# Casting GpSimd loads for r and v, regrouped input weights and a new issue order in a fused RWKV-7 and squared-ReLU MLP kernel

## The chip, the cores and the metric

The kernel runs on one core of a Trainium2 chip. The metric is the device time of one execution in microseconds. An execution is called fast or slow: slow is one more than 1.5% above the fastest of the same kernel. The profile of the kernel before that is read below was taken in an execution of 303.0 us that counted as slow in its own first set (fastest 296.8 us); in later sets nearly all its runs between 297 and 303 us counted as fast. Spans read from that profile are therefore some us longer than those of a typical fast execution (medians of about 300 to 302 us in the later sets), and the text says where that matters.

Ratios are the mean time of one kernel's fast runs over that of the other's in the same rounds on the same chip, so they are not quite the ratios of the medians quoted beside them.

In the views PE is TensorE, PEld its weight loads, DVE VectorE, ACT ScalarE, POOL GpSimd and SP SyncE; a q behind a name is the engine's sequencer, which issues DMAs. L284 is line 284 of that run's kernel. A line of the groups ends with busy us, mean ns of one instruction, and the idle time before it with what ended it. A line of the waits ends with the total us, the number of waits and the longest.

## The reference

The reference runs a recurrent attention over 768 steps for 4 x 8 heads of width 40, and feeds the result to an MLP.

```python
for t in range(S):
    y[:, :, t] = np.einsum('bhd,bhde->bhe', rt, state)
    Sa = np.einsum('bhde,bhe->bhd', state, at)
    state_decay = state * wt[:, :, None, :] - np.einsum('bhd,bhe->bhde', Sa, bt)
    state = state_decay + np.einsum('bhd,bhe->bhde', vt, kt)
# x: (3072 tokens, 320), made of y
h = x @ w_in              # 320 x 2048
r = np.maximum(h, 0.0)
out = (r * r) @ w_out     # 2048 x 320
```

## The kernel before

The kernel cuts the 768 steps into chunks of 64, and handles a chunk for two batch entries at a time: 24 groups of 128 tokens. A full group goes through 65 small operations (loads, decay sums, transposes, triangular products, state update, MLP, store). A list scheduler in the kernel places the operations of all groups from tables of priorities (`PLACE`, `FIRST`, `LAST`) and emits one instruction stream per engine. ScalarE and VectorE work their streams in order: in the trace before, all 264 ScalarE and 260 VectorE instructions of the groups start in exactly the emitted order.

All inputs come in on SyncE's queue, but for the MLP weights (GpSimd) and the first group's k and b (ScalarE). A group has twelve SyncE issues: two halves each for w, k, b, a and v, one for r, and the store of the group's output.

```python
def load(name, dst, step, src, other, deps):
    eng = "ACT" if g == 0 and name in ("LK", "LB") else "SP"
    q_ = nc.scalar if eng == "ACT" else nc.sync
    def f():
        for be in range(2):                      # two batch entries: two DMAs
            h = 1 - be if other else be
            q_.dma_start(out=V(dst, step * be, [(40, 8), (1, 40)], 64 * h, 64), in_=tok(src, b0 + be))
    add(name, g, eng, 1.3, f, deps, dma=1.05)
...
load("LV", vf, 0, v, True, [...])                # fp32 staging tile
nc.sync.dma_start(out=rf[:], in_=src)            # r, fp32 staging tile
...
nc.gpsimd.tensor_copy(out=V(rb, ...), in_=V(rf, ...))              # RC: cast r
nc.gpsimd.tensor_copy(out=V(vm, 512 * be, ...), in_=V(vf, ...))    # VC0, VC1: cast v
```

The first MLP product reads its stationary weights with a step of 16 columns, because hidden unit 16*partition + block makes the output weights contiguous to load:

```python
mm(out=V(p, 512 * s + 128 * i, [(1, 128)]), lhsT=V(WIN[x], blk, [(16, 128)]),
   rhs=xt[:, 128 * x:128 * x + 128], start=False, stop=i == 3 and x > 0)
```

## Time and profile before

| | before |
|---|---|
| time, median of the first 4 runs | 301.0 us (296.8 to 304.6) |
| span in the profile | 301.3 us |
| TensorE busy | 265.5 us, 88% |
| GpSimd busy | 131.9 us, 44% |
| SyncE issues in the trace | 284, their lengths sum to 232 us |
| DMA engines, mean share in the middle | 0.6 |

The prediction below shows the lines of this profile one by one. One reading that it did not make is added here. It is the timeline of SyncE in a calm part of the kernel before; the columns are start, length, and what was issued how often in a row.

```profile
112.35 1.28 SPq L284 DMA_DIRECT2D Vf<-in_v_dram  x2
113.68 0.63 SPq L295 DMA_DIRECT2D Rf<-in_r_dram  x1
114.35 2.42 SPq L284 DMA_DIRECT2D KBf<-in_k_dram  x2
116.87 1.54 SPq L284 DMA_DIRECT2D Af<-in_a_dram  x2
```

Each issue begins within 0.1 us of the end of the last. SyncE does not stop for a buffer or a result here; it issues without a break. Counted over the trace in stretches of 20 us, it is issuing for 18.0 to 19.1 us of each, from the first to 240 us. Its pace can be set against TensorE's: from 40 to 240 us it makes 226 issues in 199 us, twelve per 10.6 us, while TensorE in its steady part needs 10.3 us for a group. So SyncE is, by a little, the slower of the two and cannot catch up once it is late. The page's busy shares cannot show this: issuing does not count as busy. Most issues take about 0.63 us, but 63 of the 284 take over 1 us, and these make the pace; in 47 of the 63 none of the semaphores (the counters of finished work) that the issue waits for changed meanwhile, so they are no plain waits for tiles. What lengthens them stays open.

### The profile page before, as it was taken

How to read it: one execution, taken by the hardware profiler on the slowest of the kernel's cores; microseconds unless marked ns; L12 is line 12 of the kernel's file. 1: busy time of each engine (PE TensorE's matmuls, PEld its weight loads, DVE VectorE, ACT ScalarE, POOL GpSimd, SP SyncE). 2: the span in 40 equal slices, each digit the busy share in tenths (PEclk: the TensorE clock that was granted, in tenths of full speed). 3: DMA queues.
4: the chain of work that ended last, by engine and by line, in shares of the span. 5: the costliest groups of instructions: out<-in, count | busy, mean ns of one | idle time of the engine just before them, and what ended most of it. 6: DMA issues, size and time to landing. Idle time of an engine off the chain costs nothing.

```text
span 301.3 us, 13557 instructions
## 1 busy us (share of the span) xinstructions
PE 265.5 (88%) x5928; PEld 224.5 (75%) x5928; DVE 185.0 (61%) x300; ACT 147.5 (49%) x265; POOL 131.9 (44%) x245
## 2 busy tenths in 40 slices
PE   0775999985997899999999699999999889999980
PEld 0455798875886788888888688888888778888860
DVE  7235667384565557767766557766767657875520
ACT  1443164653435266556546436645644635656340
POOL 2763533853554263763644344654546325510000
PEclk9999999999697999999999979999999999999996
DMA  8899976755656566665565656555546562000000
GB/s 118 132 154 198 201 125 98 119 115 104 114 114 108 95 110 125 113 119 98 108 124 108 119 106 117 107 113 105 103 101 112 109 125 55 29 24 6 28 29 32
DMA packets 134011, 31.02 MB, mean 103 GB/s; under 512 B 127232, under 2 KB 133376, under 8 KB 133952
## 3 DMA queue, kind: packets, MB, share of 16 engines
q1 hardware_dynamic: 131184, 27.21, 48.7%
q0 software_dynamic: 656, 2.62, 4.7%
q8 instruction: 46, 0.75, 1.0%
q10 hardware_dynamic: 2112, 0.33, 0.7%
q14 instruction: 13, 0.11, 0.1%
HBM read 28.84 MB, written 3.93 MB: 109 GB/s over the span
## 4 chain that ended last, share of the span: by engine, by line
PE 62%; DMA 16%; ACT 7%; SPq 6%; issue 4%; POOL 1%; DVE 1%; ACTq 0%; POOLq 0%
PE hp L567 16%; PE fo L585 13%; DMA Wf<-in_w_dram 10%; SPq L284 5%; PE hp L558 4%; DMA out_dram<-OSB 4%; ACT RL L572 3%; PE sx L497 3%; PE cs L316 2%; PE kt L380 2%; PE vt L508 2%; PE cp L426 2%; PE eb L426 2%; PE x L463 2%; PE x L441 2%
## 5 line engine op out<-in xcount | busy, mean ns | idle before, releaser
L572 ACT ACTIVATE RL<-hp 128x1024 bf16<-128x1024 f32 x48 | 49.0, 1021 | 37.9 <-PE hp L567 37.7
L585 PE MATMUL fo<-WOUT,GT 128*128 128x320 bf16 x384 | 61.6, 305 | 1.0 <-DVE GT L576 1.0
L567 PE MATMUL hp<-XT,WIN 128*128 128x128 bf16 x768 | 62.1, 236 | 0.0
L349 POOL TENSOR_TENSOR KB<-KBf,EXN 128x320 bf16<-128x320 f32 x47 | 40.9, 875 | 44.1 <-ACT EXN L322 31.5
L567 PEld LDWEIGHTS <-WIN 128*128 128x128 bf16 x768 | 54.6, 151 | 3.7 <-issue 0.6
L576 DVE TENSOR_TENSOR GT<-RL 128x1024 bf16<-128x1024 bf16 x48 | 34.8, 726 | 26.1 <-ACT RL L572 26.0
L585 PEld LDWEIGHTS <-GT 128*128 128x128 bf16 x384 | 35.8, 100 | 13.4 <-DVE GT L576 1.4
L355 POOL TENSOR_TENSOR A<-Af,EXE 128x320 bf16<-128x320 f32 x24 | 20.7, 863 | 48.6 <-ACT EXE L338 43.6
L430 DVE TENSOR_TENSOR EBM<-eb,MASK 128x1024 bf16<-128x1024 f32 x24 | 29.3, 1223 | 7.6 <-PE eb L426 6.7
L430 DVE TENSOR_TENSOR CPM<-cp,MASK 128x1024 bf16<-128x1024 f32 x24 | 29.2, 1217 | 4.2 <-PE cp L426 4.0
L384 DVE COPY KBT<-kt 128x1024 bf16<-128x1024 bf16 x24 | 16.6, 691 | 23.4 <-PE kt L380 23.2
L590 ACT ACTIVATE OSB<-fo 128x320 f32<-128x320 f32 x24 | 10.5, 436 | 36.4 <-DMA out_dram<-OSB 23.6
L365 POOL CAST VM<-Vf 64x320 bf16<-64x320 f32 x48 | 21.6, 451 | 11.1 <-DMA Vf<-in_v_dram 8.8
L454 ACT ACTIVATE UZ<-x 64x320 bf16<-64x320 f32 x48 | 20.7, 431 | 10.8 <-PE x L449 8.9
L308 POOL TENSOR_TENSOR LLO<-LNW 128x320 bf16<-128x320 f32 x24 | 17.3, 720 | 16.1 <-ACT LNW L300 15.9
L300 ACT ACTIVATE LNW<-Wf 128x320 f32<-128x320 f32 x24 | 11.2, 465 | 23.3 <-DMA Wf<-in_w_dram 23.3
L558 PE MATMUL hp<-XT,WIN 64*128 64x128 bf16 x384 | 22.1, 235 | 0.0
L468 ACT ACTIVATE VM<-x 64x320 bf16<-64x320 f32 x48 | 20.6, 429 | 2.7 <-PE x L463 2.1
L338 ACT ACTIVATE EXE<-ce 128x328 f32<-128x328 f32 x24 | 10.6, 444 | 22.0 <-PE ce L333 20.0
L322 ACT ACTIVATE EXN<-cs 128x640 f32<-128x640 f32 x24 | 16.8, 700 | 8.9 <-PE cs L316 6.9
L489 DVE TENSOR_TENSOR STB<-st,GLM 128x640 bf16<-128x640 f32 x22 | 18.1, 824 | 4.2 <-PE st L483 4.2
L501 DVE COPY SB<-sx 128x640 bf16<-128x640 bf16 x22 | 10.8, 491 | 15.0 <-PE sx L497 15.0
(83 smaller groups left out, 480.3 us busy)
## 6 DMA issues: line engine op xcount, KB each, us to landing
Vf<-in_v_dram SPq DMA_DIRECT2D x48, 80.0 KB
Wf<-in_w_dram SPq DMA_DIRECT2D x48, 80.0 KB
Af<-in_a_dram SPq DMA_DIRECT2D x48, 80.0 KB
Rf<-in_r_dram SPq DMA_DIRECT2D x24, 160.0 KB
out_dram<-OSB SPq DMA_DIRECT2D x24, 160.0 KB
KBf<-in_k_dram SPq DMA_DIRECT2D x46, 80.0 KB
KBf<-in_b_dram SPq DMA_DIRECT2D x46, 80.0 KB
WOUT<-in_moe_w_out_dram POOLq DMA_DIRECT2D x2, 640.0 KB, 8.6
```

The costliest lines, as they stand in the source:

```text
L349: (nc.vector if g == 0 and be else nc.gpsimd).tensor_tensor(out=V(kb, 512 * be, [(64, 8), (1, 40)]), in0=V(kbf, 320 * be, [(40, 8), (1, 40)]),
L355: nc.gpsimd.tensor_tensor(out=V(at, 0, [(64, 8), (1, 40)]), in0=V(af, 0, [(40, 8), (1, 40)]), in1=V(exe, 0, [(40, 8), (1, 40)]), op=ALU.mult)
L365: nc.gpsimd.tensor_copy(out=V(vm, 512 * be, [(64, 8), (1, 40)], h, 64), in_=V(vf, 0, [(40, 8), (1, 40)], h, 64))
L430: nc.vector.tensor_tensor(out=V(dst, 0, [(64, 16), (1, 64)]), in0=V(psum(key, g), 0, [(64, 16), (1, 64)]), in1=V(MASK, 0, [(0, 16), (1, 64 ...
L454: nc.scalar.activation(out=V(uz, 320 * be, [(1, 320)], 64 * be, 64), in_=V(psum("x", g), 0, [(1, 320)], 64 * be, 64), func=ACTF.Copy, scal ...
L468: nc.scalar.activation(out=V(vm, 512 * be, [(64, 8), (1, 40)], 64 * be, 64), in_=V(psum("x", g), 0, [(40, 8), (1, 40)], 64 * be, 64), func ...
L489: nc.vector.tensor_tensor(out=V(stb, 0, [(128, 8), (64, 2), (1, 40)]), in0=V(psum("st", g), 0, [(40, 8), (0, 2), (1, 40)]), in1=V(glm, 0, ...
L558: mm(out=V(p, 512 * s + 128 * i, [(1, 128)]), lhsT=V(WIN[1 + s], blk, [(16, 128)], 64 * s, 64), rhs=xt[64 * s:64 * s + 64, 128 + 128 * s:2 ...
L567: mm(out=V(p, 512 * s + 128 * i, [(1, 128)]), lhsT=V(WIN[x], blk, [(16, 128)]), rhs=xt[:, 128 * x:128 * x + 128], start=False, stop=i == 3 ...
L572: nc.scalar.activation(out=rl[:], in_=psum(f"hp{hf}", g)[:], func=ACTF.Relu)
L576: nc.vector.tensor_tensor(out=gt[:], in0=rl[:], in1=rl[:], op=ALU.mult)
L585: mm(out=p[:, 0:320], lhsT=gt[:, 512 * s + 128 * i:512 * s + 128 * i + 128], rhs=WOUT[:, DM * blk:DM * blk + DM], start=blk == 0, stop=blk ...
```

## The change

The intent has three parts. Casting DMAs issued by GpSimd bring r and v straight into their bf16 tiles, so the fp32 staging tiles and the GpSimd casts go away, and SyncE has nine issues per group instead of twelve. The input weights are copied once on chip into contiguous columns. The issue order was searched anew, with 3 tiles for r and 4 for v. The tile of r also loses its padding: heads of 40 columns lie side by side, and the products that transpose r step by 40 columns. The cuts below are marked by three dots.

```diff
-PERIOD = 68.08
+PERIOD = 28.01
... all of PLACE, FIRST, LAST, STAY, and the PE and GpSimd entries of WINDOW are new ...
-    RB = ring("RB", 2, 512)
+    RB = ring("RB", NR, 344)          # NR = 3
-    VM = ring("VM", 3, 1024)
+    VM = ring("VM", NV, 1024)         # NV = 4
...
-        load("LV", vf, 0, v, True, [...])
-            nc.sync.dma_start(out=rf[:], in_=src)
+            nc.gpsimd.dma_start(out=rb[:, 0:320], in_=src)
-            nc.gpsimd.tensor_copy(out=V(rb, 0, ...), in_=V(rf, 0, ...))
-                nc.gpsimd.tensor_copy(out=V(vm, 512 * be, ...), in_=V(vf, 0, ...))
+            nc.gpsimd.dma_start(out=V(vm, 512 * be, [(64, 8), (1, 40)], h, 64), in_=tok(v, b0 + be))
...
-   lhsT=V(WIN[x], blk, [(16, 128)])
+   lhsT=WIN[x][:, 128 * blk:128 * blk + 128]
...
-    init("wi3", "DVE", 0.65, lambda: nc.vector.tensor_copy(out=WIN[2][0:64, :], in_=WIN[1][64:128, :]), ["wi1"])
+    def regroup(eng, i, src, p0, q0, n):
+        o = V(WIN[i], 0, [(128, 16), (1, 128)], p0, n)
+        x = V(WRAW[src], 0, [(1, 16), (16, 128)], q0, n)
+        ...
+    init("wp0", "ACT", 1.9, regroup("ACT", 0, 0, 0, 0, 128), ["wi0"])
+    init("wp1", "DVE", 2.2, regroup("DVE", 1, 1, 0, 0, 128), ["wi1"])
+    init("wp2", "ACT", 1.9, regroup("ACT", 2, 2, 64, 64, 64), ["wi2"])
+    init("wp3", "DVE", 2.2, regroup("DVE", 2, 1, 0, 64, 64), ["wi1"])
```

## The prediction

The forecast's sum is 12.7 + 9 + 1 - 1 = about 22 us, and 299.2 - 22 = 277 us. Its 56 ns are those of the transposes in the trace before. That the strided loads hold back the hp matmuls was the conclusion from this trace, 151 against 103 ns for the loads and 72.5 against 56 ns for the matmuls. In the paragraph that is cut most, "such issues" are DMA issues of GpSimd. The first rival's 1.5 us for an issue of 512 short runs is a supposition, and no trace showed it.

> **What bounds the kernel now.** I read the page first: the busy shares, then the forty slices.
>
> ```profile
> PE 265.5 (88%) x5928; PEld 224.5 (75%) x5928; DVE 185.0 (61%) x300; ACT 147.5 (49%) x265; POOL 131.9 (44%) x245
> ...
> PE   0775999985997899999999699999999889999980
> ...
> PEclk9999999999697999999999979999999999999996
> DMA  8899976755656566665565656555546562000000
> ```
>
> TensorE is the only engine near its span. It has three weak stretches: the first four or five slices (7.5 us each), where the DMA engines are the full ones; slices 10 to 13; and slice 23. In the two later ones the granted clock drops as well. To size them I cut the trace into windows of 10 us.
>
> ```profile
> 70.00:80.00 10.00, 7.05 (x137) 6.29 (x136) 4.21 (x7) 3.13 (x6) 3.97 (x9) 0.71 0.61 113
> ...
> 130.00:140.00 10.00, 10.00 (x251) 8.60 (x249) 7.23 (x11) 6.26 (x11) 5.08 (x11) 1.00 0.59 107
> ```
>
> The columns are the busy times of PE, PEld, DVE, ACT and POOL, then clock, DMA share and GB/s. A full window does 251 matmuls. From 60 to 110 us the five windows do 226+137+232+146+230 = 971 instead of 1255, so 284/25.1 = 11.3 us are lost; from 160 to 180, 363 instead of 502, 5.5 us; from 220 to 250, 713 instead of 753, 1.6 us. Up to 40 us there are 396 matmuls, 1.6 of the 24 groups of 247, worth 16.5 us, so the start costs about 23.5 us. So far that is 42 us lost; the last 10 us, with 37 matmuls, lose several more.
>
> The rest is a steady state in which the chain of waits stays on TensorE and repeats every 10.30 us:
>
> ```profile
> 125.01 1.16 PE hp L567 x16
> 126.17 0.45 PE sx L497 x8
> ...
> 131.25 0.45 PE vt L508 x8
> ...
> 133.27 0.45 PE kt L380 x8
> ...
> 135.31 1.16 PE hp L567 x16
> ```
>
> The columns are start, length, and what. The reader should compare two rates. The transposes sx, vt and kt are 128x128 weights with 128 moving columns, and take 0.45/8 = 56 ns each. The MLP matmuls hp of line 567 have exactly the same shape and take 1.16/16 = 72.5 ns. The weight loads, kept apart by shape, say why:
>
> ```profile
> L567 PEld LDWEIGHTS <-WIN 128*128 128x128 bf16 x768 | 54.6, 151 | 3.7 <-issue 0.6
> ...
> L558 PEld LDWEIGHTS <-WIN 64*128 64x128 bf16 x384 | 16.6, 151 | 1.0 <-issue 0.5
> L380 PEld LDWEIGHTS <-KB 128*128 128x128 bf16 x192 | 13.1, 103 | 3.3 <-POOL KB L349 2.0
> L508 PEld LDWEIGHTS <-VM 128*128 128x128 bf16 x192 | 13.1, 102 | 1.3
> ```
>
> WIN is read with a step of 16 elements (32 bytes) and a load takes 151 ns; contiguous loads of the same shape take 102 and 103 ns.
>
> [...] The trace has such issues only for the MLP weights, 0.57 to 0.64 us each with long rows; it shows none with 512 short runs. [...]
>
> **The change part by part.**
> *Regrouped weights.* Contiguous loads should let line 567 run at 56 ns: per group of tokens 32 x (72.5 - 56) = 0.53 us. Line 558 (64 rows, two row halves side by side) takes 0.28/8 = 35 ns; if a pair reaches the 56 ns of one full matmul it takes 28, so 16 x 7 = 0.11 us at most. I take 0.62 us per group, a period of 9.68 us, and 24 x 0.62 = 14.9 us. All of it lies on TensorE; some 85% falls in stretches where TensorE sets the pace, 12.7 us, and the rest only pays if the waits there shrink too. It adds four regroup copies once, by the kernel's own plan 1.9 + 1.9 us on ScalarE and 2.2 + 2.2 us on VectorE, and drops one of 0.69 us. They fall near 30 us, where the DMA engines are the limit; I charge 1 us.
> *r and v by GpSimd.* GpSimd loses the casts and gains three issues per group:
>
> ```profile
> L365 POOL CAST VM<-Vf 64x320 bf16<-64x320 f32 x48 | 21.6, 451 | 11.1 <-DMA Vf<-in_v_dram 8.8
> ...
> L360 POOL CAST RB<-Rf 128x320 bf16<-128x320 f32 x24 | 11.3, 471 | 4.2 <-DMA Rf<-in_r_dram 4.1
> ...
> L654 POOL DMA_DIRECT2D WIN<-in_moe_w_in_dram x3 | 1.9, 642 | 0.0
> ```
>
> That is 32.9 us off and 72 x 0.64 = 46 us on, if the cost is like that of the weights: GpSimd goes from 132 to 145 us, half of the span, beside TensorE and not on the path. Per group it has 6.0 us of work in a period of 9.7.
> SyncE loses three of its twelve issues per group. By the medians of its tiles (0.57 to 0.69 us, 284 issues) it now issues for about 181 us, and around 220 to 231 us its issues, some of over 2 us, fill the whole time. It falls to about 133 us. That is worth something because of these waits:
>
> ```profile
> ACT OSB L590 <- DMA out_dram<-OSB: 23.6, 8, 5.1
> ACT LNW L300 <- DMA Wf<-in_w_dram: 23.3, 9, 5.6
> ...
> SPq L596 <- ACT OSB L590: 36.9, 5, 10.9
> ```
>
> A load of w or a store that stands late in SyncE's order holds ScalarE, which works in order, and with it everything: the chain has the three Wf waits of 5.65, 3.08 and 5.66 us before 105 us, and the two store waits of 6.04 and 6.13 us. The DMA traffic itself stays as it was (about 5400 short packets per group, 0.6 of the engines), so bandwidth gains nothing and the start stays near its 23 us.
> *New order, and rings of 3 for r and 4 for v.* It places the shorter SyncE list, and the deeper v ring lets a load be issued a group earlier. Of the 18.4 us lost in the middle I expect half back, 9 us; this is judgement, as the order can't be read off before it runs.
>
> Sum: 12.7 + 9 + 1 (the part of the TensorE saving that shrinking waits release) - 1 = about 22 us. 299.2 - 22 = 277 us.
>
> **The rivals.**
> First, GpSimd descriptors are dear. If 512 short runs cost 1.5 us in place of 0.64, GpSimd has 7.8 us per group (48 x 0.86 = 41 us more in all) of a 9.7 us period, and its in-order list, with w's remainder LLO and the scaled keys KB behind a v load, becomes a second chain. [...] Against it: GpSimd idles over half of the span. It would eat the 9 us and a little more: 286 to 290 us.
> Second, the stalls stay, only elsewhere. Waits for w come from a ring of three and landing times of 5 us under load, and packets are not fewer; r and v also queue behind 2.6 MB of MLP weights on GpSimd's queue at the start. Then only the TensorE saving counts: 299 - 12 = 287 us.
> Third, the order is much better and all the middle stalls go: 299.2 - 14.9 - 18.4 + 1 = 267 us.
> Fourth, strided loads were not the cause, and hp stays at 72 ns. The equal shapes speak against it; then the time is 290 to 300 us.
>
> **Range and chances.** The first two rivals put the upper end at 289, the third the lower end at 265. I take 277 with 265 to 289. Faster by over 2% means under 293.3 us; it needs only half of the TensorE saving, so 0.92. Within 2%: 0.06, if GpSimd or the order spoil it. Slower: 0.02.
>
> **What would show it.** Right: weight loads of WIN at about 103 ns, 16 hp matmuls in 0.90 us, a steady period of about 9.7 us, PE busy share still the highest, GpSimd near 145 us with v issues of about 0.65 us, and shorter waits for w and for the store. Wrong: hp over 65 ns; v issues over 1.2 us or KB and LLO waiting behind them; TensorE waiting for VM; steady windows that no longer fill TensorE; or a start over 28 us.

## The result, and the profile after

The changed kernel took 275.4 us (median of 4 runs, 274.8 to 279.6) against 301.0 us; the ratio of the fast runs is 0.923 (95% interval 0.914 to 0.933). The predicted 277 us is 0.6% off. The terms of its sum are a different matter, and the profile after shows that at once. First, its page.

```profile
PE 246.7 (90%) x5928; PEld 204.8 (75%) x5928; DVE 193.7 (71%) x303; ACT 158.1 (58%) x267; POOL 148.4 (54%) x243
...
PE   0468799799999999999999999999999999999980
...
PEclk9999559999999999999999999999999999999996
DMA  8999999878979868978787887886856431000010
```

After the tenth slice or so TensorE has no weak stretch left; before there were two more behind the start. The DMA engines, though, rose from about 0.6 to about 0.8 in the middle.

The chain of waits of the kernel after, in its steady part:

```profile
121.28 1.00 PE hp L560 x16
124.92 1.00 PE hp L560 x16
...
131.16 1.00 PE hp L560 x16
```

The period is 131.16 - 121.28 = 9.88 us, against 10.30 before and 9.68 predicted. The sixteen hp matmuls take 1.00 us and not the predicted 0.90. The weight loads by shape:

```profile
L560 PEld LDWEIGHTS <-WIN 128*128 128x128 bf16 x768 | 43.8, 99 | 4.9
...
L551 PEld LDWEIGHTS <-WIN 64*128 64x128 bf16 x384 | 12.0, 95 | 1.8 <-issue 1.5
```

They fell from 151 to 99 and 95 ns, as predicted. GpSimd's new rows, in the groups by engine:

```profile
L360 POOL DMA_DIRECT2D VM<-in_v_dram x48 | 34.5, 720 | 3.4 <-DVE VM L646 2.2 <-DVE STB L482 0.9 <-PE st L476 0.4
...
L293 POOL DMA_DIRECT2D RB<-in_r_dram x24 | 13.7, 572 | 0.1
```

And the table of who waited for whom:

```profile
ACT OSB L583 <- PE fo L578: 9.7, 20, 2.2
...
ACT LNW L298 <- DMA Wf<-in_w_dram: 2.6, 2, 2.1
```

ScalarE's wait for w fell from 23.3 to 2.6 us. Its wait of 23.6 us for the store is gone from the table: what precedes the output copy now is the MLP itself. SyncE's timeline tells why, and answers the four lines shown before:

```profile
131.58 1.28 SPq L283 DMA_DIRECT2D Af<-in_a_dram  x2
135.00 1.42 SPq L283 DMA_DIRECT2D KBf<-in_b_dram  x2
136.46 1.31 SPq L283 DMA_DIRECT2D KBf<-in_k_dram  x2
138.96 1.28 SPq L283 DMA_DIRECT2D Wf<-in_w_dram  x2
```

There are gaps: 2.1 us after the first line, 1.2 us after the third. From 124 us on SyncE waits for free tiles, which means that it runs ahead of the work. Before that it issues without a break here too, though TensorE is full from about 80 us: nine issues take 8.2 us (40 to 120 us) against a period of 9.88, so it gains on TensorE. An unbroken row of issues is thus not yet a stall; by these numbers it is one when a group's issues take longer than the group (10.6 against 10.3 us before). In the whole trace SyncE issues 212 times, 169 us in all.

Where the time came from can be told by counting matmuls in the trace. Both kernels have 5928, in the same groups on average of 247. I mark the start of matmul 742 (three groups in) and of matmul 5682 (twenty groups later). The three numbers add up to the span.

| us | to matmul 742 | twenty groups | rest |
|---|---|---|---|
| before | 56.8 | 220.2 | 24.3 |
| after | 58.0 | 192.4 | 23.3 |

All of the gain in the span, 27.6 us, lies in the twenty groups (27.8). The start gained nothing. The profiled execution of the kernel before was a slow one, 2 us above the first set's median; the medians differ by 25.6 us.

### The profile page after: what moved, and what is told of

Its sections match the earlier page's. It is cut to its first block, busy times and chain, and to the rows that moved or that the text cites. A ratio compares the mean times of both kernels' runs of the same rounds, so it can differ in the third digit from the quotient of the medians.

```text
span 273.7 us, 13502 instructions
## 1 busy us (share of the span) xinstructions
PE 246.7 (90%) x5928; PEld 204.8 (75%) x5928; DVE 193.7 (71%) x303; ACT 158.1 (58%) x267; POOL 148.4 (54%) x243
## 2 busy tenths in 40 slices
DMA packets 134010, 27.08 MB, mean 99 GB/s; under 512 B 127232, under 2 KB 133376, under 8 KB 133952
## 3 DMA queue, kind: packets, MB, share of 16 engines
q1 hardware_dynamic: 102384, 19.35, 41.8%
## 4 chain that ended last, share of the span: by engine, by line
PE 84%; POOL 6%; DVE 4%; issue 3%; ACT 1%; POOLq 0%; ACTq 0%
PE fo L578 19%; PE hp L560 17%; PE kt L373 5%; PE hp L551 4%; PE vt L501 4%; PE sx L490 3%; PE st L471 3%; PE y L515 3%; PE cp L419 3%; PE eb L419 3%; PE cs L314 3%; PE x L434 2%; PE rt L390 2%; PE x L456 2%; PE ce L327 2%
## 5 line engine op out<-in xcount | busy, mean ns | idle before, releaser
L578 PE MATMUL fo<-WOUT,GT 128*128 128x320 bf16 x384 | 60.0, 299 | 0.8 <-DVE GT L569 0.8
L347 POOL TENSOR_TENSOR KB<-KBf,EXN 128x320 bf16<-128x320 f32 x47 | 42.1, 913 | 22.7 <-ACT EXN L320 18.3
L560 PE MATMUL hp<-XT,WIN 128*128 128x128 bf16 x768 | 52.5, 222 | 0.0
L560 PEld LDWEIGHTS <-WIN 128*128 128x128 bf16 x768 | 43.8, 99 | 4.9
L569 DVE TENSOR_TENSOR GT<-RL 128x1024 bf16<-128x1024 bf16 x48 | 36.1, 753 | 7.3 <-ACT RL L565 7.3
L360 POOL DMA_DIRECT2D VM<-in_v_dram x48 | 34.5, 720 | 3.4 <-DVE VM L646 2.2
L298 ACT ACTIVATE LNW<-Wf 128x320 f32<-128x320 f32 x24 | 11.2, 468 | 25.6 <-PE ce L331 19.2
L505 DVE COPY VMT<-vt 128x1024 bf16<-128x1024 bf16 x24 | 16.6, 690 | 4.7 <-PE vt L501 3.1
L551 PE MATMUL hp<-XT,WIN 64*128 64x128 bf16 x384 | 19.2, 218 | 0.7 <-issue 0.6
L366 POOL MEMSET VM<- 64x320 bf16 x40 | 14.5, 366 | 9.2 <-PE st L471 8.2
L373 PE MATMUL kt<-ID,KB 128*128 128x128 bf16 x192 | 15.9, 230 | 1.2 <-POOL KB L347 1.2
```

The lines of the kernel that those rows point to most:

```text
L347: (nc.vector if g == 0 and be else nc.gpsimd).tensor_tensor(out=V(kb, 512 * be, [(64, 8), (1, 40)]), in0=V(kbf, 320 * be, [(40, 8), (1, 40)]),
L360: nc.gpsimd.dma_start(out=V(vm, 512 * be, [(64, 8), (1, 40)], h, 64), in_=tok(v, b0 + be))
L373: nc.tensor.transpose(out=p[:, 128 * i:128 * i + 128], in_=kb[:, 128 * i:128 * i + 128], identity=ID[:])
L551: mm(out=V(p, 512 * s + 128 * i, [(1, 128)]), lhsT=WIN[1 + s][64 * s:64 * s + 64, 128 * blk:128 * blk + 128], rhs=xt[64 * s:64 * s + 64, 1 ...
L560: mm(out=V(p, 512 * s + 128 * i, [(1, 128)]), lhsT=WIN[x][:, 128 * blk:128 * blk + 128], rhs=xt[:, 128 * x:128 * x + 128], start=False, st ...
L569: nc.vector.tensor_tensor(out=gt[:], in0=rl[:], in1=rl[:], op=ALU.mult)
```

## The experiments

Theory: two things happened in the twenty groups, and they add. The contiguous weights shorten each group by about 0.41 us on TensorE (24 times that is about 10 us), and the shorter SyncE list takes out the stalls in the middle (18 us). The rivals are that the order or the deeper rings took the stalls out, that the casts were in the way, or that the weights did it all.

Twelve runs were made; e6 and e12 are the changed kernel, e3 and e7 one program. All gave correct results. The first two sets ran on one chip, the last on another.

| run | time, us | ratio to before | to 742 | twenty groups | rest |
|---|---|---|---|---|---|
| e1 strided again | 284.0 | 0.942 | 58.9 | 199.4 | 24.5 |
| e2 regroup only | 298.3 | 0.993 | 63.1 | 210.8 | 23.3 |
| e3 old order | 278.5 | 0.926 | 61.5 | 192.5 | 23.3 |
| e5 SyncE load back | 286.8 | 0.954 | 56.3 | 205.5 | 23.3 |
| e6 changed, again | 279.7 | 0.930 | 63.0 | 191.6 | 23.3 |
| e7 old order, again | 277.9 | 0.925 | 60.5 | 192.9 | 23.3 |
| e9 short rings | 276.9 | 0.921 | 56.1 | 195.0 | 23.4 |
| e8 no copies, split store | 269.4 | 0.897 | 56.5 | 191.6 | 20.5 |
| e12 changed, third | 279.5 | 0.920 | 60.4 | 191.6 | 23.3 |
| e10 queue only | 282.4 | 0.942 | 57.2 | 200.9 | 24.4 |
| e13 no copies | 271.9 | 0.908 | 54.5 | 191.8 | 23.4 |

The last run, e11, is told at its place: its profiled execution was a slow one. The time of e12 is the median of all its runs; its ratio leaves out the four that the rule calls slow. The first set had before at 300.3 us, the second at 301.9, the third at 300.2 us.

**e1: the changed kernel with strided weights.** The regroup copies are taken out of the order, nothing else moves.

```diff
-                            mm(out=..., lhsT=WIN[x][:, 128 * blk:128 * blk + 128],
+                            mm(out=..., lhsT=V(WIN[x], blk, [(16, 128)]),
-    init("wp0", "ACT", 1.9, regroup("ACT", 0, 0, 0, 0, 128), ["wi0"])
+    init("wp0", "ACT", 1.9, lambda: None, ["wi0"])
... wp1, wp2 likewise; wp3 is the plain copy of the kernel before
```

> The changed kernel, but the MLP weight loads read the columns with the step of 16 again and the regroup copies are gone; order, casting loads and rings as changed. Theory: the regrouping is worth what the steady period lost between the two traces, 10.30 - 9.89 = 0.41 us per group, so the period goes back to 10.30 us, hp matmuls follow each other after about 66 ns, and the time is 275.4 + 24 x 0.41 = 285 us (283 to 287), with no waits for w or the store come back. Rival: strided loads are not the cause, the period stays under 10.0 us and the time stays at 275 to 277 us.

It took 284.0 us. Its chain of waits in the steady part:

```profile
134.16 1.15 PE hp L560 x16
...
138.00 1.14 PE hp L560 x16
```

The hp matmuls are back at 1.15 us for sixteen, and 247 matmuls take 10.19 us against 9.79 (a full group has 253, which is why the periods read above are longer: 10.29 here, 9.89 after). The waits did not come back. So regrouping is worth 0.40 us per group, and it has nothing to do with the stalls. But against the changed kernel on the same chip (e6, 279.7 us, in another set) the whole difference is only 4.3 us and not 9.7: in its profile e1 starts 4.1 us sooner (58.9 against 63.0). It has no regroup copies, which fits, but the start of one and the same program varies by as much (see e6).

**e2: the kernel before with the regrouping alone.** The four copies stand together where the one copy stood, two on ScalarE and two on VectorE.

> The kernel before with the regrouped weights alone, in its own order. Theory: the steady period falls to 9.89 us, the waits for w and for the store in the middle stay, and the time is 299 - 9 = about 290 us (287 to 293). Rival: the waits set the pace and swallow the saving, 296 us or more. Second rival: the waits vanish by the regrouping alone, 281 us or less.

It took 298.3 us, a gain of only 0.7% (interval from 1.4% to none), and missed the theory's 290. In the profiles the twenty groups gained 9.4 us, about the theory's size (some of it is the slow execution that was profiled before), but the start lost 6.3 us. ScalarE's timeline and the chain of waits of the start say with what:

```profile
34.00 7.83 ACT L662 ACTIVATE WIN<-WRAW 128x2048 bf16<-128x2048 bf16 x2
```

```profile
39.07 1.91 DVE WIN L664
41.01 2.00 DVE WIN L664
```

Two regroup copies on ScalarE take 3.9 us each, where the kernel's plan says 1.9. The chain of waits, though, runs through the two on VectorE, 2.0 us each, which stand right behind one another. The expectation's first rival, that the middle waits swallow the saving, is not what happened: the saving is there, and the start swallows it. The stalls of the middle also stayed, as the theory said.

**e3 and e7: all parts of the change in the old order.** The kernel carries the emitted order of the kernel before as a list; the casting loads take the places of the old loads, and the casts are dropped. Many of the loads of v and r, most of them from the eleventh group on, come later than their old places, because their final tile must be free first; everything else keeps the old order. The same program ran in two sets.

> All parts of the change, but issued in the order of the kernel before, instruction group by instruction group: the casting loads of v and r stand where the old loads of v and r stood, the casts are left out. Theory A (the new order took the stalls out): stalls of some 18 us come back in the middle, 289 to 295 us. Theory B (SyncE's shorter list took them out, whatever the order): the time stays at 274 to 280 us. In between means both.

> The same program as the run with the order of the kernel before, now beside the changed kernel on one chip, to size what the order alone is worth. Theory: the order only shapes the start, where the first trace of it lost 3 us against the changed kernel, so 277 to 280 us, 0.5 to 1.5% over its yardstick. Rival: the order is worth nothing, within 0.4% of it.

It took 278.5 and 277.9 us; the stalls did not return (192.5 and 192.9 us for the twenty groups, against 192.4 and 191.6). In the second set it stood beside the changed kernel on the same chip and was 1.9 us quicker, not slower, so the theory of e7 fell. So the new order is not what took the stalls out and, on that chip, gains nothing at all.

**e5: three small issues per group put back on SyncE.**

```diff
             nc.gpsimd.dma_start(out=rb[:, 0:320], in_=src)
+            nc.sync.dma_start(out=JUNK[3 * (g % 3)][0:64, :], in_=r[b0, 0, ts, :])
                 nc.gpsimd.dma_start(out=V(vm, 512 * be, ...), in_=tok(v, b0 + be))
+                nc.sync.dma_start(out=JUNK[3 * (g % 3) + 1 + be][0:64, :], in_=v[b0 + be, 0, ts, :])
```

> The changed kernel with three small extra loads per group on SyncE (64 x 160 bytes each, into tiles nobody reads), beside its casting loads, so that SyncE issues twelve per group again while the traffic hardly grows. Theory B (SyncE's shorter list took the stalls out): waits for w and for the store come back and the time is 283 to 293 us. Theory A (the order did): the time stays under 279 us.

It took 286.8 us, inside theory B's range. The table of waits shows both old waits again:

```profile
ACT OSB L586 <- DMA out_dram<-OSB: 13.2, 3, 7.3
...
ACT LNW L300 <- DMA Wf<-in_w_dram: 7.0, 4, 2.8
```

The twenty groups take 205.5 us against 192.4; three stretches of one group each last 16.8, 12.8 and 12.2 us in place of about 9.7. The extra issues carry 9% of the bytes of r and v (3 x 10 KB of 328 KB per group), into tiles that nothing reads. The tiny issues cost SyncE as much as the large ones (a median of 0.63 us for both). Issues almost alone bring back 13 us. All of it falls before about 126 us, where twelve issues take 9.8 us, hardly less than the period of 9.9, so that a delay is not made up. Later they take 9.5 us, and TensorE runs at 9.8 us per 247 matmuls without a stall.

**e10: the kernel before with the queue of r and v moved, and nothing else.**

```diff
-            q_ = nc.scalar if eng == "ACT" else nc.sync
+            q_ = nc.gpsimd if name == "LV" else nc.scalar if eng == "ACT" else nc.sync
-            nc.sync.dma_start(out=rf[:], in_=src)
+            nc.gpsimd.dma_start(out=rf[:], in_=src)
```

> The kernel before with one thing moved: its loads of v and r are issued by GpSimd instead of SyncE, still in fp32 into the staging tiles, with the GpSimd casts kept, strided weights, old order and old rings. Theory (SyncE's issue list was the second limit, and shortening it is what removes the middle stalls): the time falls to that of the run with strided weights in the changed kernel, 284 us (280 to 288). Rival 1: the casts on GpSimd or the staging tiles held things up, and moving the queue alone gives less than half, 293 us or more. Rival 2: GpSimd with both the casts and the issues becomes the bound, over 300 us.

It took 282.4 us, as the theory said: the twenty groups fall from 220.2 to 200.9 us, close to e1's 199.4. Staging tiles, casts, order, rings and strided weights are all those of the kernel before. A window of 50 us has TensorE full again (same columns as in the prediction's windows), and GpSimd's rows show both the casts and the issues:

```profile
110.00:160.00 50.00, 49.95 (x1250) 43.19 (x1248) 36.44 (x54) 29.70 (x54) 37.76 (x69) 1.00 0.68 132
```

```profile
L284 POOL DMA_DIRECT2D Vf<-in_v_dram x48 | 33.7, 707 | 0.8 <-POOLq L681 0.8
L365 POOL CAST VM<-Vf 64x320 bf16<-64x320 f32 x48 | 21.5, 448 | 4.2 <-DMA Vf<-in_v_dram 1.7
```

GpSimd is busy for 175.8 us of 282.5 and holds little up: the longest that TensorE waits for one line of GpSimd is 5.3 us in all. So the cast in the DMA is not what pays; the other queue is. Dropping the casts frees GpSimd of 32 us that it could have spared. Taken alone, e10 leaves a rival: it also cuts the DMA packets from 134,011 to 108,667. The changed kernel keeps 134,010 packets and has no stalls either, so fewer packets are not the cause.

**e6, e9 and e12: the yardstick and the rings.** The changed kernel ran again in two sets. In e9 it has two tiles for r and three for v; a load that finds its tile taken is emitted as late as it must, some fifty operations later.

```diff
-    NL, NR, NV = 3, 3, 4
+    NL, NR, NV = 3, 2, 3
```

> The changed kernel itself, as the yardstick for the three runs beside it on the same chip: 274 to 278 us.

> The changed kernel with two tiles for r and three for v (as many as before) in place of three and four; every instruction in the changed kernel's order, only that a load of v or r and the zeroing of v's tile come as late as the freed tile forces, about two thirds of a group. Theory (the rings are needed because the casting load now lands in the final tile, with no staging tile in front of it, and takes 5.7 us to land): TensorE waits for v in each group and the time rises by 10 us or more, to 286 us or over. Rival: two thirds of a group is slack enough, 275 to 279 us.

> The changed kernel again as the yardstick of the three runs beside it: 274 to 280 us, in one of the two starts that it has shown (first 741 matmuls begun by about 58 or by about 63 us).

e9 took 276.9 us beside e6's 279.7, so the theory for e9 fell. Its steady period stayed at 9.79 us per 247 matmuls; the twenty groups as a whole cost 3 us more and the start cost less. The deeper rings are not needed for the steady part.

The yardstick itself needs care. The changed kernel has two times: 274.8 to 275.5 us in three of its first four runs and 279.6 in the fourth; 279.5 to 280.2 us in all six runs of e6; 275.0, 277.1 and four of about 279.7 us in e12. The ratios of the three sets to before, 0.923, 0.930 and 0.920, overlap in their intervals. The twenty groups are the same in all of them (191.6 to 192.4 us); only the start differs, 58.0 us in the first profile and 63.0 in e6. In the chain of waits of e6 a regroup copy stands in the start:

```profile
35.66 3.92 ACT WIN L656
...
39.63 1.89 PE hp L560 x16
```

TensorE waits for this copy before its first full-height MLP matmuls. In the first profile the same copy began at 33.4 us instead of 35.7. What picks between the starts from one execution to the next is not settled. The copies alone are not it: e11, which has none on ScalarE, took 59.9 us to matmul 742 in its slow execution.

**e8, e13 and e11: without the copies.** If hidden unit 128*block + partition stands in place of 16*partition + block, the input weights are contiguous as they arrive and the output weights come in rows of 1280 bytes. Three copies go, the fourth is a plain one.

```diff
-    wo_src = moe_w_out.rearrange("(p j) f -> p (j f)", p=128)
+    wo_src = moe_w_out.rearrange("(j p) f -> p j f", p=128)
... WIN loaded directly, wp0 to wp2 empty, wp3 the plain copy
-            nc.sync.dma_start(out=dst, in_=osb[:])        # e8 and e11 only, last two groups
+            nc.sync.dma_start(out=out[row:row + L, :], in_=osb[0:64, :])
+            nc.scalar.dma_start(out=out[row + T:row + T + L, :], in_=osb[64:128, :])
```

> An attempt at a better version: the output weights are loaded row block by row block (1280-byte runs), so that hidden unit 128*block + partition takes the place of 16*partition + block; the input weights are then contiguous as loaded and three of the four regroup copies go away, the fourth is a plain copy. The stores of the last two groups are split in two halves of 64 partitions on two queues. Theory: the regroup copies delay the start by about 4 us (ScalarE 3.9 us for one of them, and a VectorE instruction of the MLP waits 3.1 us behind another), and the last store takes 4.5 us to land; 269 to 273 us. Rival: the start is set by the loads of the first groups whatever the copies do, 274 to 276 us.

> The attempt at a better version without its split stores: row-block output weights and no regroup copies only. Theory: nearly all of the 10 us between the changed kernel and the attempt (279.7 and 269.4 on one chip) is the start, so 270 to 273 us here; the split of the last stores is worth 2 to 3 us of it. Rival: the split was most of it, 275 us or more.

> The attempt at a better version with the triangle constants (ones, the three GpSimd selects, and the VectorE copies made of them) put first in the order, ahead of the first loads of v: TensorE's first matmul waits 10.0 us for one of them. Theory: TensorE starts 2 us earlier and half of that reaches the end, 267 to 268.5 us. Rival: the loads of the first groups set the start, no change, 268.5 to 270 us.

e8 took 269.4 us beside e6's 279.7 on the same chip, a ratio of 0.897/0.930 = 0.964. The start is 6.5 us shorter and the rest 2.8 us; the steady part is the same. e13, without the split store, took 271.9 us beside e12's 279.5, and its rest is 23.4 us, so the split of the last store is worth those 2.8 us and the copies the remainder. How large that remainder is depends on which start the changed kernel takes: against the two runs of e12 that count as fast (277.1 and 275.0 us) e13 gains only 1.4%, about 4 us. e11 put the constants first in e8; TensorE then started at 6.2 us instead of 10.0, and the time was 269.0 us with a ratio of 0.896 against e8's 0.897 (different chips). Its theory fell: an earlier first matmul did not shorten the time. e8 beats both kernels.

## Why the prediction was right, and where it was not

*Contiguous weights make the hp matmuls follow each other after 56 ns.* Right. In the steady part of the trace after, successive starts lie 56 ns apart.

*"Per group 32 x (72.5 - 56) = 0.53 us."* This step was mis-sized. The 72.5 ns came from dividing 1.16 us by 16. In the trace before, the distance from start to start was 66 ns in the mean. The rest of the 1.16 us is one gap of 155 ns, from the last half-height matmul (line 558) to the first full-height one (line 567). The gap is still 148 ns after. So the saving is 32 x 10 ns plus 16 x 6 ns for line 558 (0.28 us to 0.23 for eight), 0.42 us; the periods give 10.30 - 9.88 = 0.42. Over 24 groups that is 10 us and not 14.9. e1 measured 0.40 us per group and e2 9.4 us over twenty groups (an upper figure, as said there), so this term is shown from both sides. The 56 ns hold with a weight load before each matmul: the trace after has 768 of both at line 560.

*"I charge 1 us" for the regroup copies.* Wrong in size. They take 3.9 us each on ScalarE and 2.0 to 4.4 us on VectorE. The start was longer by 6.3 us in e2, and by 4.1 us between e1 and e6; between e1 and the first profile it was not. I took the kernel's planned durations where the trace had none, and I took it that the start waits for loads alone.

*GpSimd goes to 145 us, off the path.* Right: 148.4 us. An issue of v costs 0.72 us (0.64 predicted), an issue of r 0.57. The longest issue of v took 0.86 us, so the first rival, issues of 1.5 us, is refuted. Longer issues show at the start alone. In the first profile one of GpSimd's issues of the output weights starts at 27.02 us, while a regroup copy runs on VectorE (26.63 to 28.75 us), takes 1.85 us and so ends 0.1 us after the copy. In e6 it starts 0.1 us before the copy, and again ends 0.1 us after it:

```profile
27.05 2.21 POOL L664 DMA_DIRECT2D WOUT<-in_moe_w_out_dram  x1
27.13 2.02 DVE L657 COPY WIN<-WRAW 128x2048 bf16<-128x2048 bf16 x1
```

In the kernel before, without the copies, the two issues of the output weights take 0.57 us in the mean; in e2 one that runs beside a copy on ScalarE alone takes 0.60 us. What holds the issue up is not shown. From 40 us on, with the copies done, no issue of GpSimd in the first profile takes over 0.75 us.

*SyncE issues for 181 us and falls to 133; half of the 18.4 us comes back, by judgement, with the order.* The direction was right and both sizes were wrong. Medians hid the long issues: the sums are 232 and 169 us. With nearly all of its issues in the first 250 us, at twelve per 10.6 us, SyncE was a second limit, not a list with room in which an order could be improved. That is why all the stalls went and not half, and why neither the order (e3, e7) nor the rings (e9) mattered. e10 shows it from the kernel before, e5 from the kernel after. Two of the prediction's lines were misread on the way. The 36.9 us that SyncE waited for the output copy lie after 249 us, when no load is left, and say nothing of the middle. The issues "of over 2 us" near 220 us are pairs; the longest single one there takes 1.6 us.

*"The DMA traffic itself stays as it was."* In bytes read and in packets (134,011 and 134,010), yes. In the engines' time, no: the share rose to 0.8. A packet of a casting load takes longer, 37 ns against 17.9 ns for a short SyncE packet, as worked out in the last section. It cost nothing that shows: e1 with casting loads and e10 without take 199.4 and 200.9 us for the twenty groups.

*The start stays near its 23 us.* Right in the first profile: 56.8 and 58.0 us to matmul 742. In e6, the same program, it took 63.0.

So 12.7 + 9 + 1 - 1 was, by the experiments, about 10 + 18, less what the start lost, 1 us in the first profile and up to 6 us in the other start. Two errors of 4 and 9 us in opposite directions, one of some us, and a profile some us slower than the 299.2 us reckoned from, met within 2 us of the truth. By the ratios of fast runs, which are free of the last error, the queue alone (e10) takes off 5.8% and all that remains of the change 1 to 2% more. The chance that the prediction gave to a gain over 2% was well founded, its middle partly luck.

## What to carry to other kernels

Sum the issue lengths of each DMA queue over a stretch and compare with the stretch, as is done for the engines: SyncE, which issued without gaps and needed 10.6 us for a round of work against TensorE's 10.3 us, was a limit here, even though no busy share said so. Moving a few issues to another queue with room may then pay more than any tuning of the order, as it did here: the queue alone (e10) took off 5.8%, the new order beside the old one on one chip (e6 and e7) nothing. Divide a stretch of matmuls by their number only after looking at successive starts, or a fixed gap passes for a rate: here 72.5 ns by division were 66 ns and one gap of 155 ns. A one-time copy at the start can cost several us if the chain of waits runs through it (6.3 us in e2); a layout of the other operand that needed no copy was better here (e13, by 1.4% or more).

## What else the traces measured

- SyncE's issues add up, one after the other. In the kernel before they took 0.51 us at the least and 0.82 us in the mean, 232 us in all, and moving three of twelve per group (e10) took 19 us off the twenty groups in the profiles, and 5.8% off the time by the fast runs.
- The time of casting loads in the DMA engines. The page of DMA queues of the changed kernel and of e10, same bytes read for r and v, gives it (queue, packets, MB, share of the 16 engines' time):

```profile
q0 software_dynamic: 29456, 6.56, 29.3%
```

```profile
q0 software_dynamic: 4112, 10.49, 16.2%
```

  Without 656 packets and 227 us for the MLP weights (4.7% of 16 x 301.3 us before, taken as unchanged), the casting loads are 28,800 packets in 1057 us, 37 ns each, against 17.9 ns for a short SyncE packet (41.8% of 16 x 273.7 us over 102,384). The same loads without a cast are packed into 3,456 packets and 505 us. So with the cast the engines spent twice the time on r and v; whether the conversion or the number of packets cost it, these two runs do not tell apart.
- A weight column step of 16 bf16 elements (before) cost 151 ns against 99 (after) for the load and 66 ns against 56 for the distance of the matmuls.
- Going from half-height to full-height matmuls took 155 ns from start to start before and 148 ns after, instead of 56.
- A copy of 2048 bf16 elements read at a step of 32 bytes took 3.9 us on ScalarE (first profile, e2, e6) and 2.0 us or more on VectorE (e2, e6), where a contiguous one took 0.69 us on VectorE (the plain copy of the kernel before).
